# Float16 halves for the second product of three MoE units, a second staging tile, and one copy of the search moved from VectorE to ScalarE

## The chip, the cores and the metric

The kernel runs on one core of a Trainium2 chip. Times are device microseconds of that core. Three runs of the kernel before took 1048.77, 1054.38 and 1056.56 us; the median is 1054.38.

## The reference

Three layers follow each other, on 2304 tokens (4 batches of 576).

```
scores = 0.125 * q @ k^T                 # 4 batches, 8 heads, 576 x 576, head size 64
kth    = 32nd largest score of a row
attn   = softmax(scores where scores >= kth) @ v
x      = attn, heads side by side        # 2304 x 512
h      = x @ w_in                        # w_in 512 x 2048
g      = max(h, 0) + log1p(exp(-|h|))    # = log(1 + exp(h))
x2     = g @ w_out                       # w_out 2048 x 512
e      = argmax(x2 @ w_gate)             # one of 8 experts for each token
out    = p_e * (max(x2 @ w1[e], 0) @ w2[e])   # w1 512 x 1024, w2 1024 x 512; p_e the softmax weight
```

The choice of the expert is a hard one, so x2 has to be accurate to nearly float32. w_in and w_out arrive as 64-bit numbers and are decoded on the chip.

## The kernel before

**Halves.** A float32 operand is split into a high half (rounded to the shorter type) and a low half (the rest). A product of two such operands takes three matmuls: high x high, high x low, low x high (`PASSES`, the pairs of halves of the left and of the right operand). The attention, the first product of the MoE layer (x @ w_in) and the transposed x use float16 halves. The second product (g @ w_out) is in plain float32 for units 1 to 8 and in float32r halves for units 9 and 10 (`TAIL = 9`). The expert layer uses float32r halves.

**The units.** The 18 token tiles of 128 rows are grouped into ten units (`UNITS`), numbered in the order in which attention finishes them. Units 8 and 9 hold two tiles, unit 10 one; unit 8 is the first half of batch 3, units 9 and 10 the last tiles. A unit goes through 16 blocks of d_ff (`KF`), one call of `moe_step` each. `layer1` issues the 12 matmuls of the first product for a block (L646), exp and log on ScalarE (L660, L661), and for units 9 and 10 the halves of g and of the block of w_out (`halves`: high half by a ScalarE copy, L672, low half by a VectorE subtraction, L673; the halves of g lie in the buffers `qn`, `kn`, `vn` and those of w_out in `w`). `layer2` issues the second product for a block that `layer1` has done two steps before (`GLAG = 2`): L686 in float32, L683 in halves. The exp's result `sa` has two buffers, `g` four. After the last block the two results are copied out (L690) and `route` works out expert, weight and place of each token in small steps; it ends with DMAs of the rows on SP's queue (L752) and an indirect DMA on GpSimd's queue that scatters the places (L755).

**The staging of a unit.** `unit_x` splits each tile of x into float16 halves in the staging tile `xh` (ScalarE L606, GpSimd L607) and transposes it by DMA on SP's queue (L608). `xh` has one buffer, so the second tile of a unit waits until the first has been read. It is called two blocks before the end of the unit ahead (`XAHEAD = 2`).

**The attention.** 72 groups of two (tile, head) pairs run in order: scores on TensorE (L456) into PSUM tiles `sa` and `sb`; the search for the 32nd largest score (`emit_softmax`); exponentials; a DMA transpose of the probabilities (L544, SP's queue); the product with v three groups later (`LAG`, L559 and L561). The search first sorts the scores into pairwise maxima and minima (VectorE L496 to L501), then takes four rounds of MAX8 over a row that grows from 128 to 128, 320 and 576 columns, with a MATCH_REPLACE8 between them. The 64 keys without a partner are copied unchanged into columns 256 to 319 by VectorE (L500, both tiles in one instruction, 72 in all); the third MAX8 is the first to read them. ScalarE's L502 copies the raw scores out of `sb`, which frees it for the next group. ScalarE's L529 to L532 and L540 and GpSimd's L531, L541 and L542 form the probabilities. The heads' operands are staged in the tile `st` (`prep_split`, `prep_step`), the last time some fifteen groups before the end.

**The order.** Each group of attention is followed in the program by 1.7 blocks of MoE on average (`MOER`). The order in which each engine runs its instructions is not the program's: a planner simulates the time line with its own costs, takes instructions of higher priority first and fills an engine's idle time with later work whose inputs are ready. So work of a late unit can stand early in a queue. On the chip each engine, and each DMA queue, works its list off in order.

**The expert layer** (`part_two`) runs nine slots of 256 tokens and a half slot. Slot loads are issued on SP's queue (L932 the token list, L936 and L939 the weights) and the rows are gathered by indirect DMAs on GpSimd's queue (L944); the first two slots' loads and gathers fall into the time of the last units. Its matmuls are L996 and L1009, its halves L957 and L958. `check` (L163, L164) compares sums and maxima that the first part left with limits, to choose a slower path where float16 does not suffice; its answer is read after the last slot.

## Time and profile before

| | |
|---|---|
| median of three runs | 1054.38 us (1048.77 to 1056.56) |
| the profiled execution | 1059.72 us |
| its span, first to last instruction | 1058.0 us |
| mean granted TensorE clock | 0.936 of full speed |
| TensorE busy | 885.0 us (84%) |
| VectorE busy | 849.3 us (80%) |
| ScalarE busy | 801.2 us (76%) |
| GpSimd busy | 604.0 us (57%) |

The span has three stages: the attention with decoding and the first MoE units to about 700 us, the last MoE units to about 818 us, and the expert layer to the end. Shares of the whole span mix stages with different limits, so they are read by stretch. Matmuls overlap each other and their ends are modelled: the time of a run of matmuls is best read as the distance from its start to the start of the next run. Idle time of an engine costs something only where the chain of work that ended last passes through it.

### The profile page before, as it was taken

To read this page: it belongs to the slowest core of one execution; us is meant where nothing else is said; L and a number is where in the kernel's file an instruction comes from. 1 tells how busy PE (TensorE), PEld (TensorE's weight loads), DVE (VectorE), ACT (ScalarE), POOL (GpSimd) and SP (SyncE) were. 2 spreads that over 40 slices of the span, in tenths; PEclk is the share of its full clock that TensorE was granted. 3 is DMA by queue.
4 is the path that set the end of the run, shared out by engine and by line. 5 is a ranking of instruction groups with operands and counts; after the bars stand their busy time and mean duration, and the time that the engine had idled before them with its cause. 6 is when DMAs were issued, how large, how long until landed. Compare 5 with 4: busy or idle time off the path is not lost.

```text
span 1058.0 us, 22206 instructions
## 1 busy us (share of the span) xinstructions
PE 885.0 (84%) x7146; PEld 655.0 (62%) x7146; DVE 849.3 (80%) x3021; ACT 801.2 (76%) x1866; POOL 604.0 (57%) x631
## 2 busy tenths in 40 slices
PE   1124359774998989998999999999999999999994
PEld 0013236443675656675666666676787989999993
DVE  4779999998997968996989999955356987777773
ACT  5878898988888979987998888863678555555552
POOL 3888898998767768876778777652001022111111
PEclk9986559876999989998999999999999999999998
DMA  7897799788799987669978855464301667666650
GB/s 188 193 205 189 180 192 193 179 168 172 114 131 164 138 152 129 117 80 150 152 131 120 99 90 95 72 86 131 102 12 31 170 220 243 242 212 230 237 202 23
DMA packets 295859, 156.97 MB, mean 148 GB/s; under 512 B 257524, under 2 KB 257652, under 8 KB 295732
## 3 DMA queue, kind: packets, MB, share of 16 engines
q1 hardware_dynamic: 292116, 145.73, 67.1%
q0 software_dynamic: 3616, 9.72, 2.6%
q8 instruction: 58, 0.95, 0.4%
q14 instruction: 69, 0.57, 0.2%
HBM read 77.89 MB, written 11.11 MB: 84 GB/s over the span
## 4 chain that ended last, share of the span: by engine, by line
PE 47%; DVE 13%; DMA 12%; ACT 9%; POOL 8%; issue 6%; SPq 4%; POOLq 0%; ACTq 0%; DVEq 0%
PE h L646 11%; PE h L996 9%; PE y L686 8%; PE y L1009 8%; PE y L683 3%; DVE mx L522 3%; DVE wk L518 3%; DMA xT<-xh 3%; POOL e L531 2%; POOL p L542 2%; DMA w<-in_moe_w_in_dram 2%; PE sb L456 2%; PE m L559 1%; ACT e L532 1%; PE sa L456 1%
## 5 line engine op out<-in xcount | busy, mean ns | idle before, releaser
L646 PE MATMUL h<-xT,w_in_s 128*128 128x256 f16 (+1 forms) x1920 | 228.7, 269 | 22.9 <-ACT sa L660 14.4
L686 PE MATMUL y<-w_out_s,g 128*128 128x512 f32 x480 | 229.0, 601 | 1.3 <-ACT g L661 1.2
L646 PEld LDWEIGHTS <-w_in_s 128*128 128x128 f16 x1920 | 174.9, 101 | 82.7 <-issue 52.7
L531 POOL TENSOR_TENSOR e<-s,e 128x576 f32<-128x576 f32 x144 | 204.0, 1432 | 17.7 <-ACT e L530 10.4
L522 DVE MAX8 mx<-wk 128x8 f32<-128x128 f32 (+2 forms) x432 | 200.9, 503 | 0.1
L542 POOL TENSOR_TENSOR p<-e,p 128x512 f16<-128x512 f32 x144 | 167.8, 1165 | 0.0
L456 PEld LDWEIGHTS <-q 128*128 128x128 f16 (+1 forms) x640 | 55.8, 108 | 175.4 <-issue 125.8
L518 DVE MATCH_REPLACE8 wk<-mx,wk 128x128 f32<-128x128 f32 (+1 forms) x432 | 145.1, 343 | 0.1
L686 PEld LDWEIGHTS y<-w_out_s,g 128*128 128x128 f32 x480 | 82.7, 192 | 64.0 <-issue 58.1
L976 POOL DMA_INDIRECT out_dram<-ot,idx x19 | 19.5, 1028 | 176.1 <-DVE ot L975 173.4
L532 ACT ACTIVATE e<-e,bias 128x576 f32<-128x576 f32 x144 | 110.4, 768 | 12.7 <-POOL e L531 12.2
L996 PEld LDWEIGHTS h<-xT,wf 128*128 128x128 f32 x864 | 111.8, 191 | 5.4 <-ACT wf L957 0.2
L996 PE MATMUL h<-xT,wf 128*128 128x256 f32 x864 | 113.9, 283 | 0.0
L456 PE MATMUL sa<-kt,q 128*128 128x256 f16 (+1 forms) x320 | 54.0, 302 | 71.0 <-DMA kt<-st 23.4
L1009 PE MATMUL y<-wf,hT 128*128 128x512 f32 x432 | 112.8, 398 | 0.0
L456 PE MATMUL sb<-kt,q 128*128 128x320 f16 (+1 forms) x320 | 62.7, 338 | 53.6 <-ACT s L502 53.5
L530 ACT ACTIVATE e<-s,kths 128x576 f32<-128x576 f32 x144 | 104.9, 767 | 0.8
L559 PEld LDWEIGHTS <-pT 128*128 128x128 f16 (+1 forms) x1440 | 86.8, 106 | 22.9 <-issue 19.8
L559 PE MATMUL m<-v,pT 128*128 128x65 f16 (+1 forms) x1440 | 93.9, 201 | 7.2 <-DVE xtail L586 4.3
L540 ACT ACTIVATE p<-e 128x576 f16<-128x576 f32 x144 | 97.4, 678 | 0.7
L541 POOL TENSOR_TENSOR p<-e,p 128x64 f16<-128x64 f32 x144 | 46.1, 320 | 70.4 <-ACT p L540 65.9
L1009 PEld LDWEIGHTS y<-wf,hT 128*128 128x128 f32 x432 | 76.7, 189 | 13.0
(235 smaller groups left out, 1791.1 us busy)
## 6 DMA issues: line engine op xcount, KB each, us to landing
w1r<-in_moe_w_dram SPq DMA_DIRECT2D x20, 1024.0 KB, 6.3
w2r<-in_moe_w_dram SPq DMA_DIRECT2D x20, 1024.0 KB, 7.8
w<-in_moe_w_in_dram SPq DMA_DIRECT2D x16, 512.0 KB, 4.0
w<-in_moe_w_out_dram SPq DMA_DIRECT2D x16, 512.0 KB, 4.0
rows<-xr SPq DMA_DIRECT2D x37, 128.2 KB, 3.1
qn<-in_q_dram SPq DMA_DIRECT2D x16, 288.0 KB, 4.1
kn<-in_k_dram SPq DMA_DIRECT2D x16, 288.0 KB, 6.1
vn<-in_v_dram SPq DMA_DIRECT2D x16, 288.0 KB, 3.5
```

Source lines behind the costliest of these rows:

```text
L456: last_qk[0] = nc.tensor.matmul(ps[p0:p1], lhsT=qs[:, h, r0:r1, :].rearrange("p r d -> p (r d)"), rhs=kt[:, k0:k1, cs], start=first, stop= ...
L518: nc.vector.match_replace(out=to, in_to_replace=mx[:, i, 8 * j:8 * j + 8], in_values=src[i], imm_value=NEG)
L522: nc.vector.max(out=mx[:, i, 8 * j + 8:8 * j + 16], in_=src[i])
L530: nc.scalar.activation(e[i], s[i], AF.Relu, bias=kths[:, 2 * gi + i], scale=-K_UP)
L531: nc.gpsimd.tensor_tensor(out=e[i], in0=s[i], in1=e[i], op=ALU.subtract)
L532: nc.scalar.activation(e[i], e[i], AF.Exp, bias=bt[:, i], scale=SCORE)
L542: nc.gpsimd.tensor_tensor(out=p16[:, S + D:], in0=e[i][:, 0:S - D], in1=p16[:, 0:S - D], op=ALU.subtract)
L559: nc.tensor.matmul(o[:, h, 0:D + 1], lhsT=pT(r), rhs=v16[:, h, c, 0:D + 1], start=r == 0, stop=r == R - 1)
L646: nc.tensor.matmul(hps[:, :n], lhsT=w_in_s[:, c, j, p, o:o + 128], rhs=xT[:, 0:len(u.tiles), r, c, :], start=m == 0, stop=m == 3 * KD - 1)
L686: nc.tensor.matmul(u.y[i], lhsT=g[:, cs], rhs=w_out_s[:, f, :], start=f == 0, stop=f == KF - 1)
L996: nc.tensor.matmul(h, lhsT=w1f[:, a, c, :], rhs=xT[:, b, c, :], start=n == 0, stop=n == 3 * KD - 1)
L1009: nc.tensor.matmul(y[i], lhsT=hT[g][:, a, i * 128:i * 128 + 128], rhs=w2f[:, b, :], start=g == 0 and n == 0, stop=g == KF2 - 1 and n == 2)
```

## The change

Five edits:

- The last three units (8, 9 and 10) take the second product in float16 halves: unit 8 instead of float32, units 9 and 10 instead of float32r halves.
- The halves of w_out are made once, in unit 8, and kept for units 9 and 10. Block 0 goes into the decoder's tile `t`, block f into the place of block f-1 of `w_out_s`, each float32 column giving room for two float16 numbers. The halves of g go into the `g` tile, and log overwrites exp in `sa`.
- The low halves are made by GpSimd instead of VectorE.
- The second tile of units 8, 9 and 10 is staged in the attention's `st` instead of `xh`.
- The copy of the 64 keys (L500) is made by ScalarE. The check gets the sums of |w_out|'s high halves (`y_sums`, 16 reductions on VectorE in unit 10) and a lower limit of 1 for the sums of exp.

```diff
-TAIL = 9
+HALF_Y = 8
...
-                          (e_sums, 0.0, E_MAX), (w_sums.rearrange("p a b -> p (a b)"), 64.0, 6.0e4)):
+                          (e_sums, 1.0, E_MAX), (w_sums.rearrange("p a b -> p (a b)"), 64.0, 6.0e4),
+                           (y_sums, 64.0, 6.0e4)):
...
-            nc.vector.tensor_copy(w2[:, :, PS:PS + US], ps[:, :, PS:PS + US])
+            nc.scalar.activation(w2[:, :, PS:PS + US], ps[:, :, PS:PS + US], AF.Copy)
...
-            xh = x2p.tile([128, 2, DM], F16, name="xh", bufs=XHB)
+            if i and flags is not None and units_made[0] >= HALF_Y:
+                xh = stg.tile([128, R, 2, D], F16, name="st").rearrange("p r s d -> p (r s d)")[:, 0:2 * DM]
+                xh = xh.rearrange("p (r c) -> p r c", r=2)
+            else:
+                xh = x2p.tile([128, 2, DM], F16, name="xh", bufs=XHB)
...
-        g = gp.tile([128, 256], F32, name="g")[:, :n]
+        half_y = flags is not None and u.number >= HALF_Y
+        g = a[:, :n] if half_y else gp.tile([128, 256], F32, name="g")[:, :n]
...
-        if u.number >= TAIL:
-
-            g2 = raw.tile([128, R * D], F32R, name="qkv"[f % 3] + "n")[:, :2 * n].rearrange("p (s t) -> p s t", s=2)
+        if half_y:
+            if u.number == HALF_Y:
+                w_half[f] = (dec.tile([128, C], F32, name="t") if f == 0 else w_out_s[:, f - 1]).bitcast(F16).rearrange(
+                    "p (s c) -> p s c", s=2)
+                halves(w_half[f], w_out_s[:, f])
+            if u.number == len(UNITS):
+                nc.vector.tensor_reduce(y_sums[:, f:f + 1], w_half[f][:, 0], op=ALU.add, axis=AX.X,
+                                        apply_absolute_value=True)
+            g2 = gp.tile([128, 256], F32, name="g").bitcast(F16).rearrange("p (s t) -> p s t", s=2)[:, :, :n]
             halves(g2, g)
-            w2 = dec.tile([128, 2 * C], F32R, name="w", bufs=DWB).rearrange("p (s c) -> p s c", s=2)
-            halves(w2, w_out_s[:, f, :])
-            g = g2, w2
+            g = g2
         u.g[f] = g
 
     def halves(t, src):
         nc.scalar.activation(t[:, 0], src, AF.Copy)
-        nc.vector.tensor_tensor(out=t[:, 1], in0=src, in1=t[:, 0].bitcast(F32), op=ALU.subtract)
+        nc.gpsimd.tensor_tensor(out=t[:, 1], in0=src, in1=t[:, 0], op=ALU.subtract)
...
-            if u.number >= TAIL:
+            if flags is not None and u.number >= HALF_Y:
                 for m, (a, b) in enumerate(PASSES):
-                    nc.tensor.matmul(u.y[i], lhsT=g[0][:, a, cs], rhs=g[1][:, b, :], start=f == 0 and m == 0,
+                    nc.tensor.matmul(u.y[i], lhsT=g[:, a, cs], rhs=w_half[f][:, b, :], start=f == 0 and m == 0,
```

(`flags` is not None in the fast path, which is the one that is timed.)

## Rows read from the trace of the kernel before

**Rows 1.** The chain that ended last: share of the span by engine.

```profile
PE 47%; DVE 13%; DMA 12%; ACT 9%; POOL 8%; issue 6%; SPq 4%; POOLq 0%; ACTq 0%; DVEq 0%
```

**Rows 2.** Stretches (us): length, busy PE, PEld, DVE, ACT, POOL; granted clock, DMA.

```profile
275.00:500.00 225.00, 210.04 (x1878) 141.49 (x1878) 192.86 (x815) 189.29 (x480) 167.93 (x178) 0.96 0.87 132
500.00:675.00 175.00, 171.56 (x1534) 116.21 (x1533) 165.52 (x680) 153.91 (x366) 133.38 (x144) 1.00 0.73 111
675.00:700.00 25.00, 24.23 (x207) 16.37 (x205) 24.25 (x98) 22.18 (x53) 17.17 (x19) 1.00 0.38 64
725.00:745.00 20.00, 20.00 (x115) 12.80 (x113) 11.80 (x100) 8.57 (x26) 3.10 (x3) 1.00 0.65 231
...
788.00:820.00 32.00, 30.29 (x288) 24.52 (x287) 21.30 (x87) 25.91 (x92) 3.04 (x4) 1.00 0.12 26
```

**Rows 3.** The chain in order of time: start, length (us), engine, line, count.

```profile
639.97 4.42 DMA xT<-xh
...
742.15 1.72 PE y L686 x4
...
773.07 1.40 PE y L683 x6
```

**Rows 4.** Time line, TensorE, in unit 8: start, length (us), line, tiles, count.

```profile
727.25 2.78 PE L646 MATMUL h<-xT,w_in_s 128*128 128x256 f16 x24
729.87 1.88 PE L686 MATMUL y<-w_out_s,g 128*128 128x512 f32 x4
```

**Rows 5.** Time line, ScalarE, one block of unit 9; in brackets idle time and releaser.

```profile
756.78 0.39 ACT L660 ACTIVATE sa<-h 128x256 f32<-128x256 f32 x1 [0.69 <-PE h L646]
...
757.74 0.42 ACT L672 ACTIVATE qn<-g 128x256 fp32r<-128x256 f32 x1
758.18 0.63 ACT L672 ACTIVATE w<-w_out_s 128x512 fp32r<-128x512 f32 x1
```

**Rows 6.** Subtractions by line: duration ns min/median/max, first and last start.

```profile
L673 DVE TENSOR_TENSOR w<-w_out_s,w x32: 681/692/1116, 551.5 to 816.6; 128x512 fp32r<-128x512 f32 x32
...
L607 POOL TENSOR_TENSOR xh<-x,xh x16: 1147/1161/1602, 132.7 to 725.9; 128x512 f16<-128x512 f32 x16
...
L541 POOL TENSOR_TENSOR p<-e,p x144: 295/306/752, 37.0 to 705.0; 128x64 f16<-128x64 f32 x144
```

**Rows 7.** The log instructions (L661) between 700 and 820 us.

```profile
L661 ACT ACTIVATE g<-sa x43: 293/416/419, 704.1 to 816.3; 128x256 f32<-128x256 f32 x27, 128x128 f32<-128x128 f32 x16
```

**Rows 8.** Who waited for the ScalarE halves (L672): us in total, times.

```profile
  PEld y L683: 1.2, 2
  PE y L683: 0.6, 1
```

**Rows 9.** Time line, ScalarE: a unit's second tile waits for the staging buffer.

```profile
644.50 0.63 ACT L606 ACTIVATE xh<-x 128x512 f16<-128x512 f32 x1 [2.84 <-DMA xT<-xh]
...
715.05 0.63 ACT L606 ACTIVATE xh<-xtail 128x512 f16<-128x512 f32 x1 [7.20 <-DMA xT<-xh]
```

**Rows 10.** By line: the search's copy, the exp of a block, a check's reduction.

```profile
L500 DVE COPY wk<-sb x72: 270/280/284, 20.6 to 691.3; 128x128 f32<-128x128 f32 x72
...
L660 ACT ACTIVATE sa<-h x160: 253/368/413, 152.9 to 815.4; 128x256 f32<-128x256 f32 x128, 128x128 f32<-128x128 f32 x32
...
L163 DVE TENSOR_REDUCE flx<-w_sums x2: 164/167/170, 817.5 to 817.9; 128x1 f32<-128x16 f32 x2
```

**Rows 11.** One search instruction of each group (L501), from 275 to 700 us.

```profile
L501 DVE TENSOR_TENSOR wk<-sb,s x48: 668/680/684, 275.0 to 691.5; 128x512 f32<-128x512 f32 x48
```

**Rows 12.** Time line, GpSimd's queue in the tail; in brackets idle time and releaser.

```profile
733.40 0.99 POOL L944 DMA_INDIRECT xg<-rows,idx  x1 [6.33 <-PE h L646]
...
747.07 0.94 POOL L944 DMA_INDIRECT xg<-rows,idx  x1 [11.42 <-DMA idx<-table]
...
787.12 1.00 POOL L755 DMA_INDIRECT table<-ids,dsti  x1 [37.87 <-DVE ohcum L747]
797.87 0.98 POOL L755 DMA_INDIRECT table<-ids,dsti  x1 [9.75 <-DVE ohcum L747]
```

More of the change, by code (lines that the diff above doesn't have):

```diff
@@ L144, in attn_moe_moe2 @@
     e_sums = const.tile([128, len(UNITS) * KF], F32, name="e_sums")
+    y_sums = const.tile([128, KF], F32, name="y_sums")
     w_sums = const.tile([128, DFF // C, KD], F32, name="w_sums")
@@ L181, in run @@
             late = part_one(tc, p, q, k, v, w_in, w_out, const, ident, before, ones, iota_e, reg_e, wg, ids,
-                            ohcum, done, early, table, rows, flags if halves else None, sums, w_sums, e_sums, kths)
+                            ohcum, done, early, table, rows, flags if halves else None, sums, w_sums, y_sums, e_sums, kths)
         args = w1, w2, out, ident, ones, ohcum, done, early, late, table, rows, meta, left, rare
@@ L201, in part_one @@
 def part_one(tc, ctx, q, k, v, w_in, w_out, const, ident, before, ones, iota_e, reg_e, wg, ids,
-             ohcum, done, early, table, rows, flags, sums, w_sums, e_sums, kths):
+             ohcum, done, early, table, rows, flags, sums, w_sums, y_sums, e_sums, kths):
     nc = tc.nc
@@ L587, in emit_av @@
                                 in1=rc[ps_].to_broadcast([ps_.stop - ps_.start, 2, D]), op=ALU.mult)
+    units_made = [0]
     def unit_x(tiles):
+        units_made[0] += 1
         n = 128 * len(tiles)
@@ L631, in moe_step @@
             layer2(*behind.pop(0))
+    w_half = {}
     def layer1(u):
```

## The prediction, before the result was known

> **What bounds it now.** I read three views in this order. First the chain of work that ended last, by engine: TensorE carries 47% of it, VectorE 13%, ScalarE 9%, GpSimd 8% [rows 1]; no single engine owns the span, so the next question is where TensorE owns it. Second the busy time by stretch [rows 2]: from 275 us on TensorE is busy for 210 of 225, then 172 of 175, then all of 725 to 745, at a granted clock of 1.00 from 500 on (its 2.4 GHz level). VectorE is just as full in 500 to 675 (165.5 of 175) and half idle once the attention is over. ScalarE stands at 154 of 175 there. So the attention stage has two engines at the limit and a third close to it, and the stage after it has one, TensorE. Third the pieces of the chain in the tail [rows 3]: units 8 to 10 appear as unbroken turns of first product and second product. Unit 8's second product costs 1.72 us per block of d_ff (two tiles in float32), that of unit 9, already in float32r halves, 1.40 us for its six matmuls. What TensorE no longer has to do there should come off the end.
>
> **The second product of unit 8.** Removed: 16 blocks of 1.72 us. Added: 16 blocks of six float16 matmuls of 512 columns, a size that no row shows. Upper end: as dear as float32r, 1.40 [rows 3]. Lower end: the first product's float16 matmuls of 256 columns, which pass 24 in the 2.62 us between 727.25 and 729.87 [rows 4], 0.109 each; doubled 0.218, six of them 1.31. I take the lower, the same type with only the width changed. 16 x (1.72 - 1.31) = 6.6 us off; at the upper end 5.1.
>
> The Trainium skill ("TensorE: Matmul & The Clock Gate", Back-to-back issue gap) would have a stream of load and matmul pairs at N=512 run at 131 ns each, against 216 by its formula for one alone. This trace's 0.109 for 256 columns sits with the second. By 131 ns the six would take an estimated 0.79 us; what that makes of the time is the fourth rival.
>
> **The second product of units 9 and 10.** Unit 9: 16 x (1.40 - 1.31) = 1.4; unit 10, one tile, half of it, 0.7. Together 2.1 us off, 0 at the upper end. First products do not change.
>
> **What feeds them.** For one block of unit 9 ScalarE issues exp, its sum, log, the copy of g (0.42) and the copy of w_out (0.63), then waits 0.69 for the first product [rows 5]; a block takes 2.72 there, so ScalarE needs 2.03. Unit 8 now gets this load, with 2.61 (1.31 + 1.31) per block on TensorE: cover 0.58, cost nothing once the attention is over. The low halves move from VectorE (692 ns for 512 columns) to GpSimd, where the same shape takes 1161 [rows 6]; 64 columns take 306, so 256 interpolate to 0.67. GpSimd's 1.83 per block also lies within 2.61. The cover is gone where unit 8 still meets the attention: of the 48 blocks of units 8 to 10, 43 have their log after 700 [rows 7], so five come before; in 675 to 700 ScalarE is busy 22.2 and GpSimd 17.2 of 25 [rows 2], and five blocks bring 5.3 and 9.2, over by 2.5 and 1.4. I charge 1 us; ends 0 and 2.5. Units 9 and 10 lose 32 copies of w_out on ScalarE (20 us) and all their VectorE subtractions. TensorE waited for those copies 1.2 + 0.6 us [rows 8], and unit 10's stretch, the one from 788 on, has 1.7 us without TensorE [rows 2]. I take 1.2 off; ends 0 and 3.
>
> The Trainium skill ("GPSIMD Engine Reference", Engine selection) sends elementwise work to VectorE, GpSimd being about 2x slower with two inputs. The rows give 1.68, and what matters is the cover; by the rule's 2x the block would need an estimated 2.2 us, still under TensorE's.
>
> **The mended staging.** ScalarE's copy of a unit's second tile waits until the first tile's transpose has freed the one buffer: 2.84 us at 644.5 (unit 8) and 7.20 at 715.05 (unit 9) [rows 9]. The copy now goes to a staging tile that attention has left, so both waits vanish, and with them what ScalarE holds back behind them: score copies and exponentials at 644, unit 8's exp and log at 715. TensorE and VectorE stay about full at both places, and next late is TensorE's own work. The chain passes through the first transpose with 4.42 us [rows 3]. I take 1 us off, ends 0 and 4.4. At 715 its main worth is keeping ScalarE free for unit 8's new copies, already counted as hidden above.
>
> **The search's copy.** VectorE loses 72 x 0.280 = 20.2 us, ScalarE gains 72 copies of 128 elements from PSUM; nearest row the exp of 128 columns, minimum 253 ns [rows 10]: 18.2 us. Where VectorE ends last this is a gain, where ScalarE does, a loss: by the chain's shares 13% of 20.2 off and 9% of 18.2 on, 1.0 us off. The copy is needed only by the third MAX8, two rounds of the search later, so a short delay does no harm. But it waits for the score matmuls, and behind it on ScalarE stand other groups' exponentials, for which GpSimd and then the pT transposes on SP's queue wait. Ends: 13.4 us off (first rival), 9 us on, if half of ScalarE's addition ends last.
>
> **Sums and queues.** The check gets two reductions of 16 columns (0.16 each [rows 10]) with two small compares, unit 10 gets 16 reductions of 512 columns in place of its 32 VectorE subtractions: nothing on the path, VectorE being idle for a third of that stretch. No DMA is added; two transposes on SP may start earlier. w_out's halves overwrite the weights of the block before, so they wait for unit 7's reads of that block, past by then.
>
> Sum: -6.6 - 2.1 + 1.0 - 1.2 - 1.0 - 1.0 = -10.9 us. The profiled execution took 1059.7 (span 1058.0 and 1.7 around it), so 1048.8 in its own terms. It stood 5.3 above the median 1054.4 of the runs shown; against that median I forecast 1043.5.
>
> **Rivals.** *First: the search sets the pace.* From 275 on VectorE is idle for only 32 of 225 us and 9.5 of 175. If each of the 48 groups searched after 275 [rows 11] shortens by its 0.28, that is 13.4 instead of 1.0: 1031. For it: VectorE's share of 500 to 675 (95%). Against: TensorE is at 98% there and has the same work left. *Second: unit 8's gain stays unseen.* If ScalarE and GpSimd pace its blocks at the old 3.03 us, because copies put early into unit 7's stretch delay the softmax, 6.6 and the staging's 1.0 go: 1051. The same result if the halves come about but the written order leaves TensorE waiting elsewhere. For it: ScalarE at 88% in 500 to 675. Against: the 0.69 wait in each of unit 9's blocks. *Third, slower: GpSimd's queue.* It is in order, and in the tail it held only gathers and scatters, so their waits were free: 6.33 at 733.40, 11.42 at 747.07, 37.87 at 787.12, 9.75 at 797.87, with two like the last after it [rows 12]. Now the low halves that the third pass needs stand in the same queue. TensorE can run about two blocks ahead, 5.2 us. If subtractions queue behind these waits, only what exceeds 5.2 counts: 1.1 + 6.2 + 4.6 + some 2.7 twice = 17.3, which gives 1061; with half of the long wait's excess in place of those three scatters, 1067. It decides against the change once the excess passes 10.9. Against it: the order is planned with the scatters' dependencies in it, and the long wait ends just when its tile's routing does. *Fourth: float16 at 512 columns much cheaper.* At 0.131 each the second product of unit 8 takes 0.79 per block, 14.9 off; unit 9's 9.8 and unit 10's 4.9; 29.6 instead of 8.7: 1023. The 256-column row speaks against it.
>
> **The numbers.** Chances: forecast 0.46 (its own range 1038 to 1050), first rival 0.17, second 0.20, third 0.12, fourth 0.02, other losses on ScalarE 0.03. 1% is 10.5 us, so faster means below 1043.8, which cuts the forecast about in half. Faster 0.24 + 0.17 + 0.02 = 0.43; same 0.22 + 0.20 + 0.02 = 0.44; slower 0.13. The range leaves out the fourth, most of the third and the far end of the first: 1029 to 1058.
>
> **What would show it.** Second-product pieces of 1.3 us throughout units 8 to 10; unit 8's blocks 2.6 apart, not 3.0; no wait of ScalarE for a transpose before the last three units' second tiles; ScalarE's waits for the first product still there. The search: VectorE's busy time in 500 to 675 down by some 6 us and groups closer together or not. It is wrong if the second product waits for GpSimd's subtractions, if GpSimd's waits for gathers have subtractions behind them, or if groups of the attention move apart.

## The result, and the profile after

The changed kernel takes 1069.38 us (median of four runs, 1068.34 to 1070.63); the kernel before, run beside it, 1055.47. The ratio is 1.0115 (95% interval 1.0084 to 1.0146; the two medians alone would give 1.0132): slower by 1.2%, where 1043.5 and a range up to 1058 were forecast. The profiled execution took 1070.23, its span 1068.5.

The chain of work that ended last, by engine; TensorE's share has grown from 47% [rows 1]:

```profile
PE 57%; DVE 11%; DMA 10%; ACT 7%; POOL 6%; SPq 4%; issue 3%; POOLq 0%; DVEq 0%; ACTq 0%
```

The first part of the page after, one line: busy time by engine. TensorE is busy 2.7 us less than before (885.0) in a span 10.5 longer, so its idle time has grown by 13.2 us. That is the thing to explain. Of it 2.5 us lie ahead of the start of group 57 of the attention, 2.1 between that and the start of group 71, the last one, and 8.6 behind it (the starts are given below).

```profile
PE 882.3 (83%) x7178; PEld 650.9 (61%) x7178; DVE 824.7 (77%) x2905; ACT 808.3 (76%) x1938; POOL 649.1 (61%) x695
```

Stretches of the kernel after, columns as in [rows 2]:

```profile
275.00:500.00 225.00, 209.76 (x1901) 144.26 (x1900) 191.27 (x792) 191.86 (x498) 163.27 (x176) 0.98 0.77 126
500.00:675.00 175.00, 168.98 (x1457) 112.93 (x1456) 153.14 (x616) 155.52 (x385) 141.15 (x147) 0.99 0.67 112
675.00:700.00 25.00, 24.48 (x254) 17.92 (x253) 24.49 (x99) 22.95 (x58) 20.30 (x25) 1.00 0.36 71
700.00:725.00 25.00, 23.05 (x253) 17.24 (x251) 24.49 (x106) 21.94 (x59) 21.86 (x25) 1.00 0.54 94
725.00:745.00 20.00, 13.40 (x126) 9.36 (x126) 19.32 (x97) 10.36 (x28) 12.64 (x17) 0.91 0.31 45
...
825.00:850.00 25.00, 21.09 (x114) 16.74 (x112) 13.69 (x72) 9.47 (x26) 3.27 (x5) 0.80 0.26 65
```

From 500 to 675 VectorE lost 12.4 us of work against [rows 2] and the attention did not come earlier. In 675 to 725 VectorE, ScalarE and GpSimd are all close to full: the attention, over at about 700 before, is still there. In 725 to 745, where TensorE never paused before, it is idle for 6.6 of 20 us. In 825 to 850 it is granted 0.80 of its clock on average (below).

The attention's pace shows in one instruction of each group, ScalarE's copy of the scores out of `sb` (L502 before, L504 after). The groups are numbered 0 to 71; these rows hold the fifteen from group 57 on, before and then after (duration ns, first and last start):

```profile
L502 ACT ACTIVATE s<-sb x15: 682/693/705, 577.1 to 692.2; 128x640 f32<-128x640 f32 x15
```

```profile
L504 ACT ACTIVATE s<-sb x15: 679/693/706, 591.9 to 722.7; 128x640 f32<-128x640 f32 x15
```

Group 57 is 14.8 us late, group 71 30.5. Not all of that is loss, for more of TensorE's other work is done by then. Ahead of group 57 lie three blocks of MoE more than before (92 logs against 89), some 9 us at 3.03 per block. Ahead of group 71 lie seven more (122 against 115), some 18 us by unit 8's 2.61; the rest, 12 us, is loss, and the tail does not give it back.

Time line of TensorE in unit 8, after: first and second product in turn.

```profile
742.93 1.47 PE L657 MATMUL h<-xT,w_in_s 128*128 128x256 f16 x12
744.24 1.46 PE L699 MATMUL y<-w_out_s,g 128*128 128x512 f16 x6
745.54 1.47 PE L657 MATMUL h<-xT,w_in_s 128*128 128x256 f16 x12
```

Start to start, six float16 matmuls of 512 columns take 1.30 us, a block of two tiles 2.61. Forecast 1.31 and 2.61.

**Four places where time went.** First, the waits of TensorE and VectorE for ScalarE in the search (us in total, times, longest), after, and then TensorE's before:

```profile
PE sb L458 <- ACT s L504: 88.0, 19, 10.7
...
DVE wk L503 <- ACT wk L502: 17.9, 15, 3.6
```

```profile
PE sb L456 <- ACT s L502: 53.5, 18, 6.1
```

VectorE's last sorting step (L503, the minimum) waits for the moved copy, in the written order in all 72 groups, and TensorE waits longer for a free `sb`. From VectorE's first step in a group to the copy-out, `sb` is held 4.30, 4.09 and 3.52 us before (means of groups 0 to 23, 24 to 56, 57 to 71) and 6.39, 5.11 and 4.86 after. Most of TensorE's wait lies ahead of 275 us, where it is busy only half the time: 51.3 us before, 80.7 after. Over all the kernels of this document, that wait ahead of 275 us is 75.6 to 80.7 us in the four in which the minimum waits for ScalarE (after, e2, e3, h1) and 44.7 to 51.5 in the other sixteen.

Second, lines of VectorE, GpSimd and ScalarE between 618 and 724 us, after (busy us, mean ns, idle before):

```profile
L680 DVE TENSOR_REDUCE y_sums<-w_out_s 128x1 f32<-128x512 f16 x15 | 10.1, 673 | 0.5 <-ACT w_out_s L688 0.5
```

```profile
L689 POOL TENSOR_TENSOR w_out_s<-w_out_s 128x512 f16<-128x512 f32 x15 | 17.3, 1156 | 3.2 <-ACT w_out_s L688 3.1
...
L688 ACT ACTIVATE w_out_s<-w_out_s 128x512 f16<-128x512 f32 x15 | 9.4, 627 | 1.6 <-POOL w_out_s L689 1.6
```

The planner put 15 of the 16 reductions that the program has in unit 10, and 15 of the 16 blocks' halves of w_out that it has in unit 8, among the attention's last groups, between 618 and 684 us, most of them into unit 7's time (its logs start from 612 to 673).

Third, the gap behind the last groups. Time lines of VectorE, GpSimd and TensorE, after:

```profile
725.91 6.95 DVE L795 TENSOR_SCALAR eci<-eci 128x8 int32<-128x8 int32 x1
...
732.92 0.28 DVE L588 TENSOR_TENSOR x<-m,rc 128x128 f32<-128x128 f32 x1
```

```profile
724.95 1.15 POOL L616 TENSOR_TENSOR xh<-x,xh 128x512 f16<-128x512 f32 x1
...
730.81 0.66 POOL L689 TENSOR_TENSOR g<-sa,g 128x256 f16<-128x256 f32 x1
731.44 1.39 POOL L533 TENSOR_TENSOR e<-s,e 128x576 f32<-128x576 f32 x1
```

```profile
727.18 1.46 PE L699 MATMUL y<-w_out_s,g 128*128 128x512 f16 x6
733.34 0.21 PE L561 MATMUL m<-v,pT 128*128 128x65 f16 x1 [4.71 <-DVE x L588]
```

An instruction on 8 columns takes 6.95 us on VectorE; before, the same one took this:

```profile
725.83 0.17 DVE L779 TENSOR_SCALAR eci<-eci 128x8 int32<-128x8 int32 x1
```

It ends at 732.86, within 0.1 us of the end of the ninth GpSimd instruction in an unbroken run of them (732.83). Behind it stands the normalization L588; the product with v waits for that, and behind this product, in TensorE's order, stands unit 8. I call such a standstill a hold. The Trainium skill ("SBUF — State Buffer", SBUF: two separate sides) has VectorE and GpSimd share a pair of ports under an exclusive lock, which one of them keeps for a whole instruction while the other stands still; on VectorE's side it names instructions in a two-port mode and those with two inputs in SBUF. The row agrees in kind, but nine instructions passed, not one, and no run here shows whether this one was in such a mode.

Fourth, the tail. Unit 10's routing stands alone on TensorE, after:

```profile
830.25 0.66 PE L730 MATMUL h<-ident,xr 128*128 128x128 f32 x4 [0.69 <-ACT xr L706]
831.60 1.46 PE L736 MATMUL h<-wg,x2T 128*128 128x8 f32 x8 [0.69 <-ACT x2T L732]
834.34 0.56 PE L756 MATMUL h<-oh,before 128*128 128x8 f32 x2 [1.28 <-DVE oh L753]
...
836.21 7.22 PE L1025 MATMUL y<-wf,hT 128*128 128x512 f32 x18 [0.88 <-DVE ohcum L763]
```

Before, 60 matmuls of the expert layer's first product (L996) stood between the same steps:

```profile
818.82 0.66 PE L714 MATMUL h<-ident,xr 128*128 128x128 f32 x4 [0.69 <-ACT xr L690]
819.33 3.42 PE L996 MATMUL h<-xT,wf 128*128 128x256 f32 x24
822.59 0.95 PE L720 MATMUL h<-wg,x2T 128*128 128x8 f32 x8
823.40 4.58 PE L996 MATMUL h<-xT,wf 128*128 128x256 f32 x36
```

In the kernel after, these 60 matmuls run at 800 to 813 us, among unit 10's blocks, and TensorE stands for 3.5 us in the routing, where it stood for 0.7 before. Behind these pauses its granted clock is lower: 0.71 in 830 to 835, and 0.50, the lower of its two levels (1.2 GHz), in 835 to 840. The eighteen matmuls that come next take 7.2 us (836.21 to 843.40); before, at 1.00, they took 4.3 (828.19 to 832.51). Together some 5.7 us are lost here, and not in this kernel alone. In all fifteen kernels of the table below that have float16 halves in units 9 and 10, the 60 matmuls come ahead of the routing, TensorE stands in it for 2.7 to 3.5 us, and the eighteen take 5.7 to 7.2. In the five that don't have them the 60 stand in the routing, the pauses are 0.7 to 2.1 us, and the eighteen take 4.3 to 4.4.

### The profile page after: what moved, and what is told of

It reads as the page before. It is cut to its first block, busy times and chain, and to the rows that moved or that the text cites. A ratio compares the mean times of both kernels' runs of the same rounds, so it can differ in the third digit from the quotient of the medians.

```text
span 1068.5 us, 22414 instructions
## 1 busy us (share of the span) xinstructions
PE 882.3 (83%) x7178; PEld 650.9 (61%) x7178; DVE 824.7 (77%) x2905; ACT 808.3 (76%) x1938; POOL 649.1 (61%) x695
## 4 chain that ended last, share of the span: by engine, by line
PE 57%; DVE 11%; DMA 10%; ACT 7%; POOL 6%; SPq 4%; issue 3%; POOLq 0%; DVEq 0%; ACTq 0%
PE h L657 13%; PE y L702 11%; PE h L1012 10%; PE y L1025 10%; PE y L699 3%; PE sb L458 2%; DVE mx L524 2%; PE m L561 2%; DMA w<-in_moe_w_in_dram 2%; DVE wk L520 2%; PE sa L458 2%; POOL e L533 2%; POOL p L544 2%; DMA kt<-st 1%; PE h L736 1%
## 5 line engine op out<-in xcount | busy, mean ns | idle before, releaser
L702 PE MATMUL y<-w_out_s,g 128*128 128x512 f32 x416 | 200.4, 602 | 1.2 <-ACT g L673 1.2
L1025 PE MATMUL y<-wf,hT 128*128 128x512 f32 x432 | 115.7, 406 | 0.9 <-DVE ohcum L763 0.9
L561 PE MATMUL m<-v,pT 128*128 128x65 f16 (+1 forms) x1440 | 98.2, 205 | 10.6 <-DVE x L588 5.4
L561 PEld LDWEIGHTS <-pT 128*128 128x128 f16 (+1 forms) x1440 | 90.6, 108 | 25.8 <-issue 19.7
L702 PEld LDWEIGHTS y<-w_out_s,g 128*128 128x128 f32 x416 | 71.4, 193 | 50.9 <-issue 47.5
L543 POOL TENSOR_TENSOR p<-e,p 128x64 f16<-128x64 f32 x144 | 45.6, 316 | 75.6 <-ACT p L542 70.3
L1025 PEld LDWEIGHTS y<-wf,hT 128*128 128x128 f32 x432 | 78.7, 194 | 14.8 <-DVE ohcum L763 1.0
```

The source lines that it names most:

```text
L561: nc.tensor.matmul(o[:, h, 0:D + 1], lhsT=pT(r), rhs=v16[:, h, c, 0:D + 1], start=r == 0, stop=r == R - 1)
L702: nc.tensor.matmul(u.y[i], lhsT=g[:, cs], rhs=w_out_s[:, f, :], start=f == 0, stop=f == KF - 1)
L1025: nc.tensor.matmul(y[i], lhsT=hT[g][:, a, i * 128:i * 128 + 128], rhs=w2f[:, b, :], start=g == 0 and n == 0, stop=g == KF2 - 1 and n == 2)
```

## The experiments

"VectorE copy" is the change with the 64 keys copied by VectorE as before; "behind the min" has ScalarE copy them in two instructions, one per tile, after VectorE's minimum instead of ahead of it. Ratios are to the kernel before, run beside each on the same chip. "Group 57, 71" are starts of the copy-out in the profiled execution, "blocks" the blocks of MoE whose log has started by then. "Hold" is the longest VectorE instruction with a single input between 600 and 760 us, less the shortest of its operation and shape in that trace (for the 8-column one on `eci` and L155, less the time they take when nothing holds them, 0.17 and 0.24).

| kernel | median us | ratio (95%) | group 57, 71 | blocks | hold us |
|---|---|---|---|---|---|
| before |  |  | 577.1, 692.2 | 89, 115 | 0.9 |
| after | 1069.38 | 1.0115 (1.0084 to 1.0146) | 591.9, 722.7 | 92, 122 | 6.8 |
| e1_dve_copy | 1069.61 | 1.0071 (1.0046 to 1.0096) | 585.6, 708.4 | 90, 118 | 3.2 |
| e2_act_copy_only | 1070.93 | 1.0077 (1.0049 to 1.0106) | 597.4, 718.3 | 93, 119 | 1.1 |
| e3_sums_late | 1068.74 | 1.0081 (1.0050 to 1.0112) | 596.1, 723.4 | 92, 121 | 1.2 |
| e4_copy_behind_min | 1058.24 | 0.9950 (0.9919 to 0.9982) | 578.6, 703.5 | 90, 118 | 0.7 |
| f1_behind_min_sums_late | 1070.00 | 1.0084 (1.0054 to 1.0113) | 578.9, 704.9 | 90, 117 | 5.9 |
| f2_halves_in_time | 1076.28 | 1.0116 (1.0062 to 1.0171) | 584.8, 701.0 | 90, 115 | 3.6 |
| f3_before_behind_min | 1071.96 | 1.0083 (1.0053 to 1.0112) | 585.4, 697.6 | 90, 114 | 1.0 |
| f4_dve_copy_sums_late | 1060.41 | 0.9978 (0.9955 to 1.0001) | 587.2, 703.8 | 90, 116 | 1.1 |
| g1_before_null | 1062.26 | 1.0004 (0.9973 to 1.0036) | 574.8, 689.8 | 89, 115 | 0.9 |
| g2_behind_min_sums_after_x | 1070.17 | 1.0085 (1.0055 to 1.0115) | 573.3, 701.8 | 90, 117 | 5.9, 4.8 |
| g3_dve_copy_sums_after_x | 1063.36 | 1.0018 (0.9985 to 1.0050) | 583.0, 699.6 | 90, 116 | 5.7 |
| g4_half_from_9 | 1071.85 | 1.0099 (1.0071 to 1.0128) | 587.6, 698.6 | 90, 114 | 1.1 |
| h1_load_no_wait | 1079.81 | 1.0177 (1.0129 to 1.0224) | 604.7, 735.9 | 94, 123 | 5.0 |
| i1_load_from_s | 1068.47 | 1.0065 (1.0040 to 1.0090) | 590.7, 709.2 | 89, 115 | 3.3 |
| h3_dve_copy_less_ahead | 1074.19 | 1.0137 (1.0105 to 1.0168) | 593.9, 712.0 | 90, 118 | 4.5 |
| h4_dve_copy_one_stage | 1067.88 | 1.0093 (1.0060 to 1.0125) | 583.7, 700.6 | 90, 116 | 4.5 |
| h5_behind_min_less_ahead | 1060.81 | 1.0001 (0.9977 to 1.0025) | 571.5, 693.8 | 90, 116 | 6.8, 4.6 |
| i2_before_less_ahead | 1074.98 | 1.0129 (1.0099 to 1.0159) | 588.7, 706.2 | 90, 115 | 1.1 |

**How far a new order alone moves the time.** Every edit makes the planner write a new order, so two controls come first. g1 adds an unused tile and one memset to the kernel before; i2 changes one planning constant of it.

```diff
 # g1, on before
+    y_sums = const.tile([128, KF], F32, name="y_sums")
+    nc.vector.memset(y_sums, 100.0)
 # i2, on before
-MOER = 1.7
+MOER = 1.6
```

> The kernel before with a 16 column tile more in the memory and one memset of it at the start; nothing else. It measures what a new plan of the order costs or gives by itself. If the order is as good in any plan: ratio 0.997 to 1.003. If plans differ by as much as I suspect from the runs so far: up to 1% either way, group 57 anywhere from 577 to 587 us.

> The kernel before with MOER 1.6 and nothing else: how far a new order alone moves this kernel. If the two versions with MOER 1.6 were later (+12 and +5 us) because 1.6 as such is worse: 1.004 to 1.012 of before. If orders scatter by that much whatever the edit, this one can fall anywhere in 0.990 to 1.012, and a value under 1.000 says so.

The null edit kept the time. The constant cost 1.3%, 11.6 us of them by group 57, with no operation added. So a single pair of kernels here proves little at 1%; a cause is called shown below only where a wait, a hold or an instruction in the trace carries it, or several pairs agree.

**The search's copy.** e2 makes this one edit on the kernel before, e1 undoes it in the kernel after, e4 and f3 place it behind the min (after and before).

```diff
 # e1, on after (e2 the other way round, on before)
-            nc.scalar.activation(w2[:, :, PS:PS + US], ps[:, :, PS:PS + US], AF.Copy)
+            nc.vector.tensor_copy(w2[:, :, PS:PS + US], ps[:, :, PS:PS + US])
 # e4, on after (f3 the same, on before)
-            nc.scalar.activation(w2[:, :, PS:PS + US], ps[:, :, PS:PS + US], AF.Copy)
             nc.vector.tensor_tensor(out=w2[:, :, PS + US:], in0=ps[:, :, :PS], ..., op=ALU.min)
+            for i in n:
+                nc.scalar.activation(w2[:, i, PS:PS + US], ps[:, i, PS:PS + US], AF.Copy)
```

> The changed kernel with the copy of the 64 keys back on VectorE; all else as changed. Theory A (the copy on ScalarE stands between two VectorE instructions of the same group, so the score tile sb is held longer and the groups move apart, 9 us by 275 us and 14.8 by group 57): the attention ends some 14 us earlier than in the changed kernel and the whole takes about 1055 us, 1.3% less than the changed kernel. Theory B (the copy costs nothing and all of the loss comes from the halves of unit 8 on ScalarE and GpSimd and the sums on VectorE): stays at 1067 to 1070.

> The kernel before with nothing changed but the copy of the 64 keys, which ScalarE makes. Theory A: groups as far apart as in the changed kernel up to group 57, so about 14 us over the kernel before: 1067 to 1071, ratio 1.010 to 1.016. Theory B: 1050 to 1057, ratio 0.995 to 1.002. What I forecast blind for this part alone: 1 us less.

> The changed kernel with ScalarE's copy in two instructions, one for each tile of the group, issued behind the VectorE minimum that it stood before; so VectorE's minimum no longer waits for ScalarE, and only the third MAX8 does. ScalarE makes 72 instructions of some 0.2 us more. Theory A1 (the wait between the two VectorE instructions is what the copy costs): 1053 to 1058, as with the copy on VectorE or better. A2 (what costs is ScalarE's added load, whoever waits): 1068 to 1075.

> The kernel before with ScalarE's copy alone, in two instructions behind VectorE's minimum; no float16 second product, no other staging. If VectorE's search sets the pace of the attention (my first rival: 48 groups by 0.28 us): 10 to 14 us less, ratio 0.987 to 0.991. If TensorE sets it: 0.996 to 1.002.

The one edit alone makes the kernel before slower by 0.8%. Two more pairs have the same sign: with the sums late, 0.9978 with VectorE copying and 1.0081 with ScalarE (f4, e3, under "The sums"), and 1.0071 and 1.0115 with the change otherwise whole (e1, after), though the intervals of these two overlap. Group 57 starts at 592 to 597 us in the three kernels with the copy ahead of the min (after, e2, e3), 92 or 93 blocks begun by then. It starts at 573 to 585 with the copy behind the min (e4, f1, f2, g2) and at 583 to 588 with VectorE copying (e1, f4, g3, g4), 90 blocks begun in each. Putting the copy behind the min brings group 57 forward in all three pairs, but the end in one. e4 is the best kernel of the study, 0.995 of before, 1.6% less than after by the two ratios; f1 against e3 (1.0084 and 1.0081) and f3 against e2 (1.0083 and 1.0077) stand still. In f1 a burst of sums and a hold (below) may be why; for f3 the trace does not say. e1 regained less than expected; the sums were still in the attention.

Is it ScalarE's load or the wait? h1 takes the VectorE-copy kernel g3 (under "The sums") and lets ScalarE copy 48 columns more per tile, into a scratch tile that nobody reads; i1 reads them from `s` in SBUF instead of `sb` in PSUM.

```diff
 # h1, on g3
             nc.vector.tensor_copy(w2[:, :, PS:PS + US], ps[:, :, PS:PS + US])
+            nc.scalar.activation(scratch, ps[:, :, PS:PS + 48], AF.Copy)
 # i1, in its place
+            nc.scalar.activation(scratch, s2[:, :, :48], AF.Copy)
```

> As the version with the copy on VectorE and the sums behind the last normalization (1.0018 of before), plus one more ScalarE copy of 2x48 columns per group from PSUM into a scratch tile that nobody reads: ScalarE's load without the hand-off in the middle of VectorE's work. Theory one (ScalarE's load itself holds the attention's last groups): groups 57 to 71 take 124 to 128 us as in the versions with ScalarE copying behind the min, end 1.006 to 1.010 of before. Theory two (what costs there is the wait for the copy's result, not the load): they stay at 115 to 118 us and the end within 0.999 to 1.004.

> As h1, but ScalarE's extra copy reads 2x48 columns of s in SBUF in place of the score tile sb in PSUM: the same load (72 copies of about 0.24 us) into the same scratch tile that nobody reads, and in the written order VectorE's min now stands right behind its copy with no wait for ScalarE. Theory one (the loss is the hand-off that comes with two engines reading one PSUM tile in turn): group 57 back from 604.7 to 583 to 587 us, the last fourteen groups at 115 to 120 us, end 1.002 to 1.006 of before. Theory two (ScalarE's load costs): group 57 at 595 or later, last fourteen at 124 us or more, end 1.010 to 1.018.

h1 turned out not to be free of the wait. Waits of VectorE in h1:

```profile
DVE wk L505 <- ACT scratch L504: 19.5, 12, 5.1
```

In its written order the minimum waits for ScalarE in every group, though nothing reads the scratch tile and the two instructions share nothing but the PSUM tile they read. In i1 that wait is gone from the order and the trace; the load is a little more (276 ns for one copy in the mean, 239 in h1). The fifteen groups in h1 and in i1:

```profile
L506 ACT ACTIVATE s<-sb x15: 682/699/716, 604.7 to 735.9; 128x640 f32<-128x640 f32 x15
```

```profile
L506 ACT ACTIVATE s<-sb x15: 682/692/732, 590.7 to 709.2; 128x640 f32<-128x640 f32 x15
```

From VectorE's first step to the copy-out, `sb` is held 6.22, 5.76 and 5.13 us in h1 and 4.38, 3.92 and 3.54 in i1 (means of groups as above). So what holds the score tile longer is the wait that comes with two engines reading one PSUM tile in turn, not the load. I had first put it down to the two interleaved writes into `wk`; h1 has no such write.

What the wait costs is less sure. h1 is 14.0 us behind i1 at group 57 and 26.7 at group 71, but it has begun five and eight blocks more by then, some 15 us at 3.03 and 21 at 2.61 per block, and TensorE's idle time until group 71 differs by 6.7 us. Behind group 71 h1 has a hold of its own (5.0 us, the 8-column instruction on `eci` at 739.90), and TensorE then stands for 5.38 us until 749.21. So 1.0177 against 1.0065 is the wait and that hold together. The load is not free either: i1 against g3 is 0.5% slower and 7.7 us later at group 57 (590.7, where 583 to 587 was expected without the wait); its last fourteen groups take 118.5 us (g3 116.6).

**The sums.** e3, f1 and f4 issue the reductions only behind the last search; g2 and g3 only behind the last normalization.

```diff
 # e3 (on after), f1 (on e4), f4 (on e1); g2 (on e4) and g3 (on e1) with last_x, the last L588
+                with tc.issue_after(last_dve[0].ins):
                     nc.vector.tensor_reduce(y_sums[:, f:f + 1], w_half[f][:, 0], ...)
```

> The changed kernel with the 16 reductions of w_out's high halves queued on VectorE behind the last search instruction of the attention, so that they can't be planned into it. Theory C (15 reductions of 0.67 us, 10.1 us, stand on a full VectorE between 618 and 724 us and push the last groups apart): 1058 to 1061, about 9 us less than the changed kernel. Rival: ScalarE and GpSimd, which also get unit 8's halves there, hold the groups apart anyway: 1066 to 1070.

> The changed kernel with the copy back on VectorE and the reductions late: the float16 second product with its staging, without the two edits that load or stop the search. If the second product's 8.7 us on TensorE come off the end: ratio 0.988 to 0.993. If the attention's end sets the end and the second product's gain becomes idle time of TensorE: 0.996 to 1.002.

> The changed kernel with two edits: ScalarE's copy in two instructions behind VectorE's minimum, and the 16 reductions queued behind the last search. Theory C (the reductions cost on the full VectorE what they take there, 10 us, once the search sets the pace): 0.6 to 0.9% under the version with the first edit alone, ratio to before 0.985 to 0.990. Rival (ScalarE and GpSimd hold the last groups apart): ratio 0.993 to 0.998, as without the second edit.

> ScalarE's copy in two instructions behind VectorE's minimum, and the 16 reductions queued on VectorE behind the last normalization of the attention's output (L588), not only behind the last search. In the run with the reductions right behind the last search they stood for 10 us between a reciprocal's input and the last three groups' normalizations. Theory E (reductions cost when they stand in front of the attention's last results, wherever that is): ratio 0.983 to 0.991, groups 57 to 71 in 115 to 120 us, no TensorE gap of 7 us behind the last group. Rival (a new plan decides, not the place of the sums): 0.995 to 1.008.

> The copy back on VectorE and the reductions behind the last normalization: only the float16 second product, its halves and its staging are left of the change. If the second product's gain reaches the end once nothing stands in the search: 0.988 to 0.994. If the halves on ScalarE and GpSimd in the last groups eat it: 0.997 to 1.004.

With the copy on VectorE, moving the sums out gives what the trace said: the last fourteen groups take 122.8 us with them (e1) and 116.6 without (f4, g3; before 115.1), and the ratio falls from 1.0071 to 0.9978 and 1.0018. Part of the 6 us is other work: e1 begins 28 blocks of MoE between the two groups, f4, g3 and before 26. With the copy ahead of the min the ratio falls from 1.0115 to 1.0081 (e3), within the intervals, where 9 us were expected. With the copy behind the min it goes the other way, 0.995 to 1.0084 and 1.0085. In f1 part of that is the edit itself, VectorE in f1:

```profile
709.56 0.15 DVE L586 TENSOR_SCALAR rc<-m 128x2 f32<-128x2 f32 x1
709.62 0.68 DVE L682 TENSOR_REDUCE y_sums<-t 128x1 f32<-128x512 f16 x1
710.21 7.21 DVE L682 TENSOR_REDUCE y_sums<-w_out_s 128x1 f32<-128x512 f16 x12
717.33 0.16 DVE L588 RECIPROCAL rc<-rc 128x2 f32<-128x2 f32 x1
```

The reductions went as one burst between two steps of a normalization. The other part, and g2's, I put down to holds (f1's is 5.9 us); VectorE and GpSimd in g2, the two holds and the GpSimd instructions with which they end:

```profile
639.41 6.11 DVE L755 TENSOR_SCALAR oh<-iota_e,nm 128x8 f32<-128x8 f32 x1
...
706.87 5.04 DVE L155 TENSOR_SCALAR flags<-flags 128x144 f32<-128x144 f32 x1
```

```profile
644.35 1.14 POOL L691 TENSOR_TENSOR w_out_s<-w_out_s 128x512 f16<-128x512 f32 x1
...
710.43 1.39 POOL L534 TENSOR_TENSOR e<-s,e 128x576 f32<-128x576 f32 x1
```

They end at 645.52 and 711.91, the unbroken runs of GpSimd at 645.49 and 711.82. e4 ran the second of these instructions in 0.24 us:

```profile
708.63 0.24 DVE L155 TENSOR_SCALAR flags<-flags 128x144 f32<-128x144 f32 x1
```

It was through at the first boundary between two GpSimd instructions (708.74), in a run that pauses only at 709.89; what decides which boundary lets it in, the traces do not say. Behind a hold stand searches and normalizations, so I take it to cost about its length where the attention is still the pace. That would make g2's 10.7 us of holds most of its distance to e4 (14 us by the ratios), but no run takes the hold away alone, and g3, with one of 5.7, ends at 1.0018.

**The halves of w_out.** f2 is f1 with each block's halves of w_out queued behind unit 8's own exp, so that they leave unit 7's time.

> As the version with both edits, and in addition the halves of a block of w_out queued on ScalarE behind unit 8's own exp of that block, so that they cannot be planned into unit 7's stretch. Theory D (15 copies of 0.63 us and 15 subtractions of 1.16 us, planned early, hold up the softmax of groups 57 to 71): another 3 to 6 us less. Rival: they fill idle time there, and put off they stand in unit 8's own way: 0 to 5 us more.

The last groups came down to 116.2 us, with 25 blocks begun between them (f1: 126.0 and 27), and the whole did not get faster than f1 (1.0116 and 1.0084, with intervals that overlap). TensorE is busy 17.4 of 25 us in 700 to 725, but not because products wait for halves of w_out: 5.77 us of its idle time end with VectorE's L756, itself held for 3.6 us (708.98 to 712.78). No wait of TensorE for a half of w_out stands in the trace behind 680 us. One more of 3.35 us, at 755.11, comes by way of GpSimd's queue: a gather waits 4.43 us for its tokens there (751.60), a subtraction stands behind it, exp needs the buffer that this reads, and the first product waits for exp. So the run does not say what the halves' place is worth.

**The second product of unit 8, and the staging.** g4 is g3 with `HALF_Y = 9` (unit 8 back in float32), h4 is g3 without the second staging tile.

```diff
 # g4, on g3
-HALF_Y = 8
+HALF_Y = 9
 # h4, on g3
-            if i and flags is not None and units_made[0] >= HALF_Y:
+            if False:
```

> As the one with the copy on VectorE and the sums behind the last normalization, but with float16 halves only in units 9 and 10; unit 8 in float32 as before, so no halves beside the attention's last groups apart from those planned early. If unit 8's halves are what holds groups 57 to 71 apart: those groups in 115 us as before (10 less than with them) and ratio 0.992 to 0.998, by the 2.1 us of units 9 and 10 and a shorter ScalarE. If not: groups as far apart as in the changed kernel, 1.000 to 1.006.

> As the same VectorE-copy version, without the second staging tile (the second tile of units 8 to 10 is staged as before). Prediction's step (the staging is worth 1 us, at most 4.4): end 1.002 to 1.006 of before. Rival (it is worth nothing, or its transposes start earlier and displace others): 0.998 to 1.002.

Unit 8's float16 is worth 8.6 us by the two ratios (1.0099 to 1.0018; 6.6 forecast), the staging tile 8.0 (1.0093 to 1.0018; 1 forecast, 4.4 at most). Both are no larger than what a new order alone did in i2, but in h4 the trace carries it. ScalarE and TensorE in h4:

```profile
714.87 0.63 ACT L615 ACTIVATE xh<-xtail 128x512 f16<-128x512 f32 x1 [7.71 <-DMA xT<-xh]
```

```profile
716.58 2.72 PE L657 MATMUL h<-xT,w_in_s 128*128 128x256 f16 x12 [7.37 <-ACT sa L672]
```

The same wait of ScalarE, 7.20 us, stood in the kernel before [rows 9] and cost TensorE nothing. Here unit 8's products are shorter and need ScalarE, and TensorE stands for 7.37.

**More work left for the tail.** h3 (on g3) and h5 (on e4) set `MOER` to 1.6, to fill TensorE's gap behind the last groups.

> As the same VectorE-copy version, with MOER 1.6 in place of 1.7: less expert-free MoE work is put among the attention's groups and more is left for the tail. Theory one (the second product's 8.7 us are lost because unit 8's shorter backlog leaves TensorE without ready work behind the last groups): the 725 to 750 stretch closes up, the end falls by 4 to 8 us to 0.994 to 0.998. Theory two (the gain is lost elsewhere, unit 10's routing standing alone, or the attention itself): the end stays at 1.000 to 1.006.

> The best version so far (the whole change with ScalarE's copy in two instructions behind the min, 0.995) with MOER 1.6. If more work left for the tail fills TensorE behind the last groups: 0.988 to 0.993, faster than both kernels. If the gap there is set by the last groups' own chain of softmax: 0.995 to 1.002.

Neither closed it: h3 has TensorE busy 19.8 us of 25 in 725 to 750, h5 19.5 in 700 to 725. In both a hold of 4.5 us or more on L155 lies in that stretch or just ahead of it. h3's attention is late as i2's is, but h5's, with the same constant, has the earliest group 57 of all (571.5), so the constant alone does not explain it.

## Why the prediction was wrong, point by point

**The bounds** were read rightly: TensorE is at its limit from 275 us on, with VectorE beside it until the attention ends. What was missed is that the engines take turns in each group: TensorE's next scores wait for ScalarE's copy-out, and that for VectorE's minimum, so a wait of VectorE for ScalarE is handed on to TensorE.

**The second product** is right as a price: 1.30 us for six matmuls, not 1.40 and not what the fourth rival needed, and TensorE's work is less. "Should come off the end" failed: with copy and sums put back the two kernels stand at 0.9978 and 1.0018 of before, not the 0.992 that 8.7 us would make. Against g4 unit 8's part of it is there. Where it goes can be read in the tail: TensorE's idle time behind the start of group 71 is 18.8 to 29.1 us in the fifteen kernels with the new second product and 15.1 to 17.3 in the five without. Unit 10's routing alone, with the lower clock behind it, takes 3.3 to 5.7 us more in each of the fifteen than in the kernel before. The prediction read units 8 to 10 as "unbroken turns" and did not ask which matmuls filled the routing.

**"What feeds them"** failed. ScalarE's and GpSimd's share of a block does lie under TensorE's 2.6 us, once the attention is over. But I let five blocks' halves fall into the attention's time and charged 1 us; the planner put 15 blocks of w_out there. And I moved the subtractions to GpSimd by duration alone. With GpSimd at 21.9 of 25 us in 700 to 725 it has runs without a pause, during which some VectorE instructions stand still: 6.8 us in the kernel after, 10.7 in g2 and 11.4 in h5 by two of them, at most 0.9 in the same stretch before. No row of before showed a hold of that length; the longest of the whole trace came to 1.2, and the prediction gave this cost no term at all.

**The mended staging** is right in its mechanism and too small: 8 us in g3's setting. I put that down to the cover: what hid 7.20 us before was the float32 product that the same change shortens. In the kernel after only one such wait is left, 3.94 us, at 599.91 in an earlier unit.

**"The search's copy"** is the step that failed most. It said the copy is needed only by the third MAX8, so "a short delay does no harm". The minimum right behind it waits for it, in all 72 groups, because both read one PSUM tile. That the groups of the attention move apart, the prediction's own sign of being wrong, is what came. Instead of 1.0 us off, the step is slower by 0.8% alone (e2), some 8 us, near the 9 that stood as the dear end. That end was charged to ScalarE's load; the traces show the wait instead (`sb` held longer in all four kernels that have it), and the load beside it (i1, 0.5%). How much of the 0.8% is which stays open, since putting the copy behind the min gave the time back in one pair of three.

**"Sums and queues"** failed too: the reductions are "in unit 10" in the program and in unit 7's time in the order. 10.1 us on a full VectorE: taken out, they give 0.9 and 0.5% where VectorE copies (e1 against f4, g3), and no clear gain elsewhere.

**The rivals.** The first, the search setting the pace, has something: behind the min, with the rest alike, group 57 comes 7.0, 8.3 and 9.7 us earlier than with VectorE copying (e4 and e1, f1 and f4, g2 and g3), of the 16 us that VectorE saves by then (58 x 0.28); f3 against before goes the other way. The second, the gain unseen because early copies delay the softmax, names part of what happened, without the sign. The third got the sign by another mechanism. The waits of its gathers are short after, this one the longest, and no subtraction behind them made TensorE wait:

```profile
767.96 0.96 POOL L960 DMA_INDIRECT xg<-rows,idx  x1 [3.42 <-DMA idx<-table]
```

In the kernel after, GpSimd did harm by what it does to VectorE, not by its queue; in two of the runs the queue did, once each, what this rival said: a gather waits for its tokens (5.64 us in g4, 4.43 in f2), a subtraction stands behind it, and TensorE waits 2.5 us in g4 and 3.35 in f2.

**What stays open.** Why the copy behind the min gains nothing on the kernel before (f3) and with the sums late (f1), and so the price of the wait apart from ScalarE's load; what makes kernels with the same operations differ by 12 us at group 57 (i2); the price of the holds, and what ends one: they are read from traces and were not taken away by themselves; and whether unit 10's routing would be covered again if the expert layer's first product were kept for it, which no run tried.

## What to carry to other kernels

Before moving an instruction to another engine, look at its neighbours in the program and ask which of them touch the same PSUM tile: an instruction put between two of one engine's makes the engines meet in every round, and that can matter more than its own 0.27 us. Look up where the planner will put work that is ready early, since work that is written late and has its inputs early lands on whichever engine seems free, here the fullest one. When work goes to GpSimd, count not only its time but the pauses it leaves. And when work is taken off an engine, look at what the planner then pulls forward, and which gap that had been filling.

## What the runs showed of the hardware that was not expected

VectorE instructions with one input in SBUF stood still while GpSimd worked without a pause. L155, 144 columns, took 0.24 us in e4, 5.04 in g2 and 4.71 in h4; the one on 8 columns 0.17 before and 6.95 after. In all the traces thirteen such instructions behind 600 us took over 3 us. Each ended within 0.1 us of the end of a GpSimd instruction; in eight cases, h4's among them, it was the last before GpSimd paused, in five (the 6.95 us among them) GpSimd went on. In e4 it was the first that ended. VectorE's MAX8, beside the same load, kept its time: 747 ns in the mean for 576 columns before, 746 after.

TensorE's clock fell behind pauses of about a microsecond: in unit 10's routing, after it had stood for 0.69, 0.69 and 1.28 us between small steps, the granted clock was 0.50 in 835 to 840, and six matmuls of 512 columns in the expert layer took 2.73 us instead of the 1.45 before.
